# Retention followed by a GELU MLP on one core: output matmuls one MLP step later, v scaled a stage sooner, and a reordered start

## The chip, the cores and the metric

The kernel runs on one core of a Trainium2 chip. The metric is the time of one execution on the device in microseconds; the profile's span is about 1.7 us shorter than the time of the same execution.

## The reference

```python
# q, k, v: (8, 8, 576, 64); w_in: (512, 2048); w_out: (2048, 512)
def attention(q, k, v):
    scores = np.matmul(q, k.transpose(0, 1, 3, 2)) / np.sqrt(64)
    gamma = 1.0 - 2.0 ** (-5.0 - np.arange(8))
    rel = pos[:, None] - pos[None, :]
    Dmat = np.where(rel >= 0, gamma[:, None, None] ** rel, 0.0)
    return np.matmul(scores * Dmat, v)

x = attention(q, k, v).transpose(0, 2, 1, 3).reshape(4608, 512)
h = x @ w_in
g = 0.5 * h * (1.0 + erf(h / sqrt(2)))
out = g @ w_out
```

## The kernel before

The attention is done in 40 chunks of up to 128 positions (5 per batch, the last of each has 64). The decay is folded into v (`dv`) and into the result (`dq`), and what earlier chunks contribute is carried in a state `u`. TensorE does the chunks in pieces between the steps of the MLP. An MLP step is 4 matmuls of 512 columns, 0.863 us.

The names of the pieces: T turns q and k (on TensorE for chunks 0 to 8, by a DMA transpose for the others), R is the chunk's scores (tile `sc`), S its output matmuls (into `o_ps`) and its state update (`u_ps`), U the cross part (q times the state, into the same `o_ps`), X the transpose of the result for chunks 0 to 8 (`x_ps`).

```python
ps_sc  = ... bufs=2   # scores
ps_out = ... bufs=1   # o_ps: ONE buffer
ps_u   = ... bufs=1
ps_mlp = ... bufs=3

def turn(i):                      # T, chunks 0 to 8
    ...
    nc.scalar.copy(qkT[:, 1, :, :cs], ps[:, 1, :, :cs])          # k on ACT
    nc.vector.tensor_copy(qkT[:, 0, :, :cs], ps[:, 0, :, :cs])   # q on DVE

def masked(i, sc):                # DVE, after the scores
    for e in range(2):
        ...                       # ret[e] = sc[e] * mask
    vh = ...                      # vh = v * dv
    nc.vector.tensor_tensor(vh[:cs], loaded[i][1][:cs], dv[...], op=ALU.mult)

def evacuate(i):                  # DVE: x = o_ps * dq, frees o_ps
    ...
```

The order of all this is fixed when the program is built: a planner keeps an estimate `now` of TensorE's time, issues whichever piece of attention is due, and fills in MLP steps otherwise.

```python
elif kind == "R":
    sc = scores(i)
    ...
    if open_ is not None:
        cross(open_)              # the cross part of the chunk before
    masked(i, sc)                 # DVE: ret, ret, vh
    at["S", i] = now + 1.5        # S is due two MLP steps later
    if open_ is not None:
        close(open_)              # DVE: x of the chunk before, after ret, ret, vh
elif kind == "S":
    inner(i)                      # needs ret, vh, and o_ps, that is x of the chunk before
    ...
```

## Time and profile before

| | before |
|---|---|
| time, median of 3 | 338.66 us (338.36 to 339.65) |
| span of the profiled run | 337.3 us |
| TensorE (PE) busy | 309.6 us, 92% |
| idle before `o_ps` for DVE's x, PE's waits | 9.8 us, 17 times |

These lines are of the page of the kernel before: busy time by engine, then the busy share in 40 slices of the span (9 is 90% or more), the granted TensorE clock and the DMA engines' share.

```profile
span 337.3 us, 6099 instructions
PE 309.6 (92%) x2494; PEld 163.2 (48%) x2494; DVE 101.1 (30%) x183; ACT 144.8 (43%) x284; POOL 112.0 (33%) x144
PE   6879998877999999999999999999999999999995
PEclk9799999999999999999999999999999999999999
DMA  9999999999999999999979799836421120111011
```

TensorE is the bottleneck, with weaker stretches in the first quarter. The DMA engines are 90% busy or more until about 168 us. The waits of PE in the kernel before follow, an excerpt of the view (engine, line, what released it: us in total, times, the longest).

```profile
PE o_ps L236 <- DVE x L264: 9.8, 17, 0.6
PE x_ps L278 <- DVE x L264: 4.9, 5, 1.5
PE sc_1451 L208 <- DMA qkT<-qk_ld: 1.1, 1, 1.1
PE sc_1318 L208 <- DMA qkT<-qk_ld: 0.8, 1, 0.8
PE sc_1233 L208 <- DMA qkT<-qk_ld: 0.5, 1, 0.5
```

Next, one chunk of the steady state in the kernel before, from PE's timeline (start, duration, operation, and in brackets the idle time before it) ...

```profile
189.49 0.28 PE L256 MATMUL o_ps<-u_sb,qkT 64*128 64x64 bf16 x8
189.70 0.39 PE L303 MATMUL oT<-w_out_177,g_2606 128*128 128x512 bf16 x1
...
191.01 0.38 PE L303 MATMUL oT<-w_out_183,g_2674 128*128 128x512 bf16 x1
191.22 0.38 PE L303 MATMUL oT<-w_out_183,g_2681 128*128 128x512 bf16 x1
192.23 0.19 PE L236 MATMUL o_ps<-vh,ret_2795 128*128 128x64 bf16 x1 [0.63 <-DVE x L264]
```

... and what DVE does in the same stretch.

```profile
189.69 0.69 DVE L217 TENSOR_TENSOR ret_2795<-sc_2777,msk 128x512 bf16<-128x512 f32 x1 [6.23 <-PE sc_2778 L208]
190.29 0.68 DVE L217 TENSOR_TENSOR ret_2797<-sc_2778,msk 128x512 bf16<-128x512 f32 x1
190.89 0.68 DVE L221 TENSOR_TENSOR vh<-v_ld,dv 128x512 bf16<-128x512 bf16 x1
191.49 0.68 DVE L264 TENSOR_TENSOR x<-o_ps,dq 128x512 bf16<-128x512 f32 x1
```

The four DVE operations start 0.60 us apart; the output matmuls at 192.23 wait for the last one, x, which frees the one `o_ps`. Between the scores and that moment PE has only two MLP steps, eight matmuls.

The idle column says 0.63 us. But eight matmuls that start 0.216 us apart would be done issuing at 189.70 + 8 × 0.2158 = 191.43, and the next group starts at 192.23: that is 0.80 us of lost starts. The idle column counts from the modelled end of the last matmul (191.22 + 0.38 = 191.60), and a matmul's duration of 0.38 us is longer than the 0.216 us after which the next may start. The views also print no idle time under 0.15 us, so that a wait counted from start to start has to pass about 0.3 us before it shows at all.

### The profile page before, as it was taken

Reading aid. Unit: us, or ns where it says so; the run is one execution under the profiler, and the core shown is the slowest. Engines: PE = TensorE matmul, PEld = TensorE weight load, DVE = VectorE, ACT = ScalarE, POOL = GpSimd, SP = SyncE. Lnnn points to the kernel's source line nnn. Section 1 sums busy time; section 2 is a strip of 40 time slices with the busy share of each in tenths; the row PEclk is TensorE's granted clock in tenths of the full one; section 3 lists DMA queues with packets and bytes.
Section 4 is the critical chain, followed back from the end, with each engine's and each line's share of the span. In section 5 each row is a group of like instructions: output and inputs, shape, how many; then the busy total and the mean of one; then the engine's idle time right before and its main releaser. Section 6 shows DMA issues by size and latency. Waiting matters only on the chain.

```text
span 337.3 us, 6099 instructions
## 1 busy us (share of the span) xinstructions
PE 309.6 (92%) x2494; PEld 163.2 (48%) x2494; DVE 101.1 (30%) x183; ACT 144.8 (43%) x284; POOL 112.0 (33%) x144
## 2 busy tenths in 40 slices
PE   6879998877999999999999999999999999999995
PEld 2568645765544444444444444444444444444442
DVE  1751236456242223322252222322253222000000
ACT  5368425755324641464136423642354236424711
POOL 9957878544462373243334322200000000000000
PEclk9799999999999999999999999999999999999999
DMA  9999999999999999999979799836421120111011
GB/s 139 154 191 186 185 144 191 143 138 142 156 137 173 191 147 154 174 181 109 134 137 136 54 154 159 96 57 111 109 33 23 64 79 18 23 62 64 0 61 64
DMA packets 168492, 39.40 MB, mean 117 GB/s; under 512 B 157584, under 2 KB 163984, under 8 KB 168464
## 3 DMA queue, kind: packets, MB, share of 16 engines
q0 software_dynamic: 115792, 17.97, 79.6%
q1 hardware_dynamic: 52528, 20.92, 34.1%
q8 instruction: 19, 0.31, 0.4%
q10 hardware_dynamic: 144, 0.13, 0.1%
q14 instruction: 9, 0.07, 0.1%
HBM read 36.70 MB, written 9.44 MB: 137 GB/s over the span
## 4 chain that ended last, share of the span: by engine, by line
PE 70%; DVE 16%; DMA 7%; issue 5%; ACT 2%; DVEq 0%; SPq 0%; ACTq 0%
PE oT L303 30%; PE hT L290 28%; DMA qkT<-qk_ld 6%; DVE vh L221 5%; PE o_ps L236 4%; DVE x L264 4%; PE u_ps L242 2%; DMA k_101<-in_k_dram 1%; ACT qkT L197 1%; PE x_ps L278 1%; PE qk_ps L196 1%; PE o_ps L256 1%; DVE qkT L198 1%; PE warm L403 0%; ACT L172 0%
## 5 line engine op out<-in xcount | busy, mean ns | idle before, releaser
L316 ACT COPY o_sb<-oT 128x512 f32<-128x512 f32 x35 | 20.3, 586 | 77.4 <-PE oT L303 77.4
L131 POOL DMA_DIRECT2D v_ld<-in_v_dram x39 | 33.0, 845 | 55.2 <-DVE vh L221 27.5
L131 POOL DMA_DIRECT2D qk_ld<-in_q_dram x39 | 33.3, 855 | 31.7 <-DMA qkT<-qk_ld 19.3
L131 POOL DMA_DIRECT2D qk_ld<-in_k_dram x39 | 33.1, 848 | 15.1 <-DMA v_ld<-in_v_dram 13.2
L246 ACT CAST u_sb<-u_ps 128x512 bf16<-128x512 f32 x32 | 18.7, 585 | 41.4 <-PE u_ps L242 41.4
L264 DVE TENSOR_TENSOR x<-o_ps,dq 128x512 bf16<-128x512 f32 (+1 forms) x40 | 27.3, 683 | 7.7 <-PE o_ps L256 4.3
L221 DVE TENSOR_TENSOR vh<-v_ld,dv 128x512 bf16<-128x512 bf16 x31 | 21.1, 682 | 0.0
L208 PEld LDWEIGHTS <-qkT 64*128 64x128 bf16 (+1 forms) x320 | 9.2, 97 | 19.3 <-issue 12.5
L290 PE MATMUL hT<-xT,w_in_164 128*128 128x512 bf16 (+3 forms) x96 | 17.8, 326 | 0.5 <-ACT g_1133 L294 0.5
L290 PE MATMUL hT<-xT,w_in_156 128*128 128x512 bf16 (+3 forms) x96 | 18.2, 326 | 0.0
L290 PE MATMUL hT<-xT,w_in_160 128*128 128x512 bf16 (+3 forms) x96 | 18.1, 326 | 0.1
L290 PE MATMUL hT<-xT,w_in_158 128*128 128x512 bf16 (+3 forms) x96 | 17.9, 326 | 0.2 <-ACT g_1211 L294 0.2
L290 PE MATMUL hT<-xT,w_in_166 128*128 128x512 bf16 (+3 forms) x96 | 17.9, 326 | 0.0
L290 PE MATMUL hT<-xT,w_in_170 128*128 128x512 bf16 (+3 forms) x96 | 17.7, 326 | 0.1
L290 PE MATMUL hT<-xT,w_in_162 128*128 128x512 bf16 (+3 forms) x96 | 17.7, 326 | 0.0
L290 PE MATMUL hT<-xT,w_in_168 128*128 128x512 bf16 (+3 forms) x96 | 17.6, 326 | 0.1
L312 DVE COPY o_sb<-oT 128x256 f32<-128x256 f32 x1 | 0.4, 424 | 46.5 <-ACT o_sb L311 46.5
L242 PE MATMUL u_ps<-vh,qk_ld 128*128 128x128 bf16 x128 | 12.6, 222 | 0.0
L290 PEld LDWEIGHTS <-w_in_168 128*128 128x128 bf16 x96 | 8.7, 98 | 6.7 <-issue 0.2
L290 PEld LDWEIGHTS <-w_in_164 128*128 128x128 bf16 x96 | 8.6, 98 | 6.8 <-issue 0.6
L290 PEld LDWEIGHTS <-w_in_170 128*128 128x128 bf16 x96 | 8.6, 98 | 6.6 <-issue 0.2
L290 PEld LDWEIGHTS <-w_in_160 128*128 128x128 bf16 x96 | 8.5, 98 | 6.6 <-issue 0.2
(782 smaller groups left out, 626.3 us busy)
## 6 DMA issues: line engine op xcount, KB each, us to landing
out_dram<-o_sb SPq DMA_DIRECT2D x35, 256.0 KB, 2.3
qk_ld<-in_q_dram POOLq DMA_DIRECT2D x31, 128.0 KB, 8.1
qk_ld<-in_k_dram POOLq DMA_DIRECT2D x31, 128.0 KB, 7.8
v_ld<-in_v_dram POOLq DMA_DIRECT2D x31, 128.0 KB, 8.4
qk_ld<-in_q_dram POOLq DMA_DIRECT2D x8, 64.0 KB, 8.4
qk_ld<-in_k_dram POOLq DMA_DIRECT2D x8, 64.0 KB, 8.2
v_ld<-in_v_dram POOLq DMA_DIRECT2D x8, 64.0 KB, 7.5
qkT<-qk_ld SPq DMA_TRANSPOSE x31, 7.6
```

What stands on the lines that cost most here:

```text
L131: nc.gpsimd.dma_start(dst[:cs], src[b, :, c0:c0 + cs, :].rearrange("h s d -> s h d"))
L196: nc.tensor.transpose(ps[:, j, hp, :cs], qk[:cs, j, 2 * hp:2 * hp + 2, :], ident[:cs, :cs])
L197: nc.scalar.copy(qkT[:, 1, :, :cs], ps[:, 1, :, :cs])
L208: nc.tensor.matmul(sc[e][:cs, hp, :cs], lhsT=qkT[sl, 1, hp, :cs], rhs=qkT[sl, 0, hp, :cs], start=True, stop=True)
L221: nc.vector.tensor_tensor(vh[:cs], loaded[i][1][:cs], dv[:cs, :, ci:ci + 1].to_broadcast([cs, H, D]), op=ALU.mult)
L236: nc.tensor.matmul(ov[:, e, hp, :], lhsT=s["ret"][e][:, hp, :], rhs=s["vh"][:, 2 * hp + e, :], start=(hp == 0), stop=(ci == 0 and hp == HP ...
L242: nc.tensor.matmul(u_ps[0][:, hp, :], lhsT=loaded[i][0][:cs, 1, 2 * hp:2 * hp + 2, :], rhs=s["vh"][:cs, 2 * hp:2 * hp + 2, :], start=(ci = ...
L246: nc.scalar.copy(u, u_ps[0])
L264: nc.vector.tensor_tensor(x.rearrange("p hp e d -> p e hp d")[:cs], by_parity(s["o_ps"])[:cs], dq.rearrange("p (hp e) c -> p e hp c", e=2) ...
L290: nc.tensor.matmul(hT[:, :hi - lo], lhsT=w[:, cc, o:o + 128], rhs=xT[:, cc, tok0 + lo:tok0 + hi], start=(cc == 0), stop=(cc == N_DM - 1))
L303: nc.tensor.matmul(oT, lhsT=g_tiles[t, m][:, ts * 128:(ts + 1) * 128], rhs=w_out_sb[m // 2][:, m % 2, :], start=(m == 0), stop=(m == N_DF ...
L316: nc.scalar.copy(o_sb, oT)
```

## The change

Its intent is to remove the waits of the steady state (a third MLP step ahead of the output matmuls, and vh out of the DVE chain), and to shorten the dependent chain of the first chunks, before MLP work is there to fill in.

```diff
+    warm_act = const_pool.tile([128, 1], FP32, name="warm_act")   # moved up, ahead of the loads
+    nc.scalar.activation(warm_act, ln_scale, AF.Gelu)
...
-    dma_clock = [2.4]
+    dma_clock = [2.0]
...                                    # the planner's estimates of load times
-        dma_clock[0] = max(dma_clock[0], now) + 2.75 * cs / C
+        dma_clock[0] = max(dma_clock[0], now) + 3.0 * cs / C
...                                    # and 1.3 -> 1.38 for a weight tile, twice
             nc.scalar.copy(qkT[:, 1, :, :cs], ps[:, 1, :, :cs])
-            nc.vector.tensor_copy(qkT[:, 0, :, :cs], ps[:, 0, :, :cs])
+            if i in (1, 2):
+                nc.scalar.copy(qkT[:, 0, :, :cs], ps[:, 0, :, :cs])
+            else:
+                nc.vector.tensor_copy(qkT[:, 0, :, :cs], ps[:, 0, :, :cs])
+            scaled_v(i)
...
+    def scaled_v(i):                  # was the end of masked()
         vh = ...
...
-        if open_ is not None and (nxt["R"] == N_CH or (open_ < N_PE_TR and r_at > now + 1.2)):
+        if open_ is not None and (nxt["R"] == N_CH or open_ < 4 or (open_ < N_PE_TR and r_at > now + 1.2)):
...
                 inner(i)
                 nxt["S"] += 1
+                if N_PE_TR <= i + 1 < N_CH:
+                    scaled_v(i + 1)
...
-                at["S", i] = now + 1.5
+                at["S", i] = now + (1.5 if i < 4 else 2.5)
```

More of the change, by code (lines that the diff above doesn't have):

```diff
@@ L145, in load_w_in @@
         w_in_sb.append(t)
-        dma_clock[0] += 1.3
+        dma_clock[0] += 1.38
         land_in.append(dma_clock[0] + 0.8)
@@ L155, in load_w_out @@
         w_out_sb.append(t)
-        dma_clock[0] += 1.3
+        dma_clock[0] += 1.38
         land_out.append(dma_clock[0] + 0.8)
@@ L169 @@
         load_chunk(i)
-    warm_act = const_pool.tile([128, 1], FP32, name="warm_act")
-    nc.scalar.activation(warm_act, ln_scale, AF.Gelu)
     st = {i: {} for i in range(N_CH)}
@@ L219, in masked @@
             st[i]["ret"].append(r)
+    def scaled_v(i):
+        b, ci, c0, cs = chunks[i]
         vh = vh_short if cs < C else v_pool.tile([128, H, D], BF16, tag="vh", name="vh")
```

## The prediction

> **What bounds the kernel.** TensorE work: the page's busy table gives PE 309.6 of 337.3 us (92%). In the pure MLP stretches that end the chain of waits, 64 matmuls of 512 columns take 13.81 us, 215.8 ns each; the Trainium skill, "TensorE: Matmul & The Clock Gate", section "Wait — 56ns, not 53.3ns?", has 215.7 ns for a warm array. The MLP cannot be packed tighter; only PE gaps can go. In PE's timeline the gaps over 0.1 us sum to about 22.5 us:
> - 0 to 22 us: 6.9 (waits on DVE or ACT, the largest 1.48 and 1.05 for x, 1.39 for qkT);
> - 22 to 62 us: 2.75 (x_ps behind x 1.05 and 1.16; qkT 0.27 twice);
> - 62 to 90 us: 4.1 (qkT transposes by DMA 2.4; x 1.08; ACT's 64-column gelus 0.67);
> - 90 to 290 us: fifteen waits of o_ps for DVE x, 0.49 or 0.63 each, 8.75 in sum.
>
> **Steady state.** After a chunk's scores DVE runs ret, ret, vh, x (0.60 us each, start to start). PE fills this with two MLP steps (8 matmuls, 1.73 us), then waits for x, because o_ps has one buffer. The change takes vh out of that chain (-0.60) and puts a third MLP step (0.86 us) ahead of the output matmuls. Slack becomes about +0.8 us, so all fifteen waits vanish: -8.7 us. vh runs in DVE's idle time (DVE 30% busy).
>
> **First chunks.** Gelu's table load (1.28 us) moves ahead of the k cast into idle ACT time: ACT's k copy starts near 6.65 instead of 7.32. With vh off the ret chain, q copies of chunks 1 and 2 on ACT (0.58 instead of 0.42, but not behind DVE's queue), and cross closing each chunk before the next scores, I follow the durations through: chunk 1's output matmuls at about 13.5 (before 14.69), chunk 2's 16.5 (18.46), first MLP matmul 17.8 (19.46), chunk 3's output matmuls 19.8 (22.22) with equal MLP work done: -2.4 us. Landings in the trace (v of chunk 3 at 15.6; w_in from 16.9 to 26.5) just allow it.
>
> **Middle.** x_ps waits shrink from 2.2 to about 0.9, the two x waits (1.08) go: -2.4 us. But until about 150 us the DMA engines are 90% busy or more, and a qkT transpose lands 8 to 11.5 us after issue. The new order puts chunks 9 to 13 later in PE's work, about as much as PE gains, so qkT waits stay at 2 to 3 us. The 64-column gelus now run sixteen in a row: +0.4.
>
> **Sum (an estimate from these durations):** 338.7 - 8.7 - 2.4 - 2.4 + 0.5 = 325.7 us.
>
> Predicted 325.8 us, range 323.0 to 329.5 (8 in 10). Chances: faster by over 2% 0.95, within 2% 0.05, slower by over 2% 0.0.
>
> **What would show it.** PE busy stays near 309 us, its share rises to about 95%. In the waits, o_ps behind x falls from 9.8 us to under 0.5. In the timeline the first hT matmul starts near 17.8, chunk 3's output matmuls near 19.8. The tail of three pure MLP stages keeps its length. vh leaves the chain of waits (5.0% before).
>
> **What would make it wrong.** (1) DMA: if qkT doesn't land earlier, the middle keeps its absolute time and up to 4 us of early gains turn into qkT waits (330). (2) DVE runs in order: vh moved sooner can block it until v lands. (3) The half-clock stretch (8.56 to 11.97) may vanish or lengthen: about 0.6 us. (4) A later x could delay xT; I read ample lead.

## The result, and the profile after

The changed kernel takes 317.39 us (median of 4 runs, 317.04 to 318.05) against 338.62 us before (median of 4, one more than in the first table). The ratio is 0.937, with a 95% interval of 0.9345 to 0.9395. All ratios here are the mean time of one kernel's runs over that of the other's of the same rounds, so not quite the ratio of the medians. The gain is 21.2 us where 12.9 were predicted, and the time lies outside the predicted range.

The same lines of the page, for the kernel after:

```profile
span 316.3 us, 6068 instructions
PE 302.2 (96%) x2460; PEld 164.1 (52%) x2495; DVE 100.0 (32%) x181; ACT 145.0 (46%) x286; POOL 112.2 (35%) x144
PE   7889998999999999999999999999999999999995
PEclk9999999999999999999999999999999999999999
DMA  9999999999999999999999999804340221110011
```

35 matmul records are missing from this trace (2460 matmuls for 2495 weight loads), so its PE busy time is not to be compared with the other. PE's waits in the kernel after, again an excerpt:

```profile
PE x_ps L284 <- DVE x L270: 0.7, 2, 0.4
PE hT L296 <- DMA w_in_160<-in_moe_w_in_dram: 0.7, 1, 0.7
PE sc_1578 L211 <- DMA qkT<-qk_ld: 0.6, 1, 0.6
PE sc_1699 L211 <- DMA qkT<-qk_ld: 0.5, 1, 0.5
```

The wait of `o_ps` for x is gone from the list. The same chunk in PE's timeline of the kernel after (one of the twelve matmuls has no record) ...

```profile
175.59 0.28 PE L262 MATMUL o_ps<-u_sb,qkT 64*128 64x64 bf16 x8
175.81 0.39 PE L309 MATMUL oT<-w_out_179,g_2608 128*128 128x512 bf16 x1
...
178.19 0.38 PE L309 MATMUL oT<-w_out_194,g_2751 128*128 128x512 bf16 x1
178.41 0.19 PE L242 MATMUL o_ps<-vh,ret_2799 128*128 128x64 bf16 x1
```

... and DVE's part of it, where vh comes last and nobody waits for it:

```profile
175.79 0.69 DVE L220 TENSOR_TENSOR ret_2799<-sc_2781,msk 128x512 bf16<-128x512 f32 x1 [5.91 <-PE sc_2782 L211]
176.40 0.68 DVE L220 TENSOR_TENSOR ret_2801<-sc_2782,msk 128x512 bf16<-128x512 f32 x1
177.00 0.68 DVE L270 TENSOR_TENSOR x<-o_ps,dq 128x512 bf16<-128x512 f32 x1
177.59 0.68 DVE L227 TENSOR_TENSOR vh<-v_ld,dv 128x512 bf16<-128x512 bf16 x1
```

From 175.81 to 178.41 are 2.60 us for twelve matmuls, and 12 × 0.2158 is 2.59: no start is lost.

Where did 21 us come from? I lined up the two traces with the programs' order of matmuls and, for each stretch, took the distance between the starts of its groups less what the matmuls need at their undisturbed spacing (0.2158 us at 512 columns, 0.109 at 256, and so on). This counts every lost start, whatever the modelled ends say.

| term | predicted, us | measured start to start, us |
|---|---|---|
| output matmuls' waits after 87 us (26 in the kernel before) | -8.7 | -13.6 (13.9 to 0.3) |
| start, to the end of the first MLP stage | -2.4 | -2.6 (37.60 to 34.95) |
| output matmuls' waits in the middle | -1.1 | -2.0 (2.0 to 0.0) |
| `x_ps` waits in the middle | -1.3 | -1.5 (2.5 to 1.0) |
| waits for landings of qkT and of q | 0 | -1.2 (2.9 to 1.7) |
| 64-column stage, bound by ACT | +0.4 | -0.7 (2.1 to 1.4) |
| sum | -13.1 | -21.6 (spans: -21.0) |

The terms overshoot the spans by 0.6 us: small ones that are not listed go the other way, such as 0.35 us between the first two score matmuls of one chunk at 64.50 us in the kernel after. The 0.3 that is left of the first term is 0.01 us at each group, as in e2 below, and no wait.

The largest error is the first line. The profile booked the 26 late waits of the kernel before as fifteen: ten of 0.63 us and five of 0.49. Start to start they are ten of 0.80, five of 0.67, five of 0.32 and six of 0.15 us, 13.9 us in all. The five of 0.32 leave 0.15 us of idle time, just under what the views print, and the six of 0.15 leave none.

### The profile page after: what moved, and what is told of

It is laid out like the page before. It is cut to its first block, busy times and chain, and to the rows that moved or that the text cites. A ratio compares the mean times of both kernels' runs of the same rounds, so it can differ in the third digit from the quotient of the medians.

```text
span 316.3 us, 6068 instructions
## 1 busy us (share of the span) xinstructions
PE 302.2 (96%) x2460; PEld 164.1 (52%) x2495; DVE 100.0 (32%) x181; ACT 145.0 (46%) x286; POOL 112.2 (35%) x144
## 4 chain that ended last, share of the span: by engine, by line
PE 86%; DMA 6%; POOL 3%; ACT 2%; issue 1%; DVE 1%; ACTq 0%
PE hT L296 39%; PE oT L309 36%; DMA qkT<-qk_ld 3%; PE o_ps L242 3%; DMA w_in_160<-in_moe_w_in_dram 2%; PE u_ps L248 2%; POOL qk_ld L134 2%; PE o_ps L262 2%; POOL v_ld L134 1%; ACT o_sb L322 0%; PE x_ps L284 0%; PE qk_ps L195 0%; DVE x L270 0%; ACT qkT L196 0%; DVE qkT L200 0%
## 5 line engine op out<-in xcount | busy, mean ns | idle before, releaser
L134 POOL DMA_DIRECT2D qk_ld<-in_q_dram x39 | 33.4, 856 | 50.7 <-DMA qkT<-qk_ld 18.3
L211 PEld LDWEIGHTS <-qkT 64*128 64x128 bf16 (+1 forms) x320 | 9.4, 97 | 16.3 <-issue 12.7
```

What stands on the lines that cost most here:

```text
L134: nc.gpsimd.dma_start(dst[:cs], src[b, :, c0:c0 + cs, :].rearrange("h s d -> s h d"))
L211: nc.tensor.matmul(sc[e][:cs, hp, :cs], lhsT=qkT[sl, 1, hp, :cs], rhs=qkT[sl, 0, hp, :cs], start=True, stop=True)
```

## The experiments

Three theories are set against each other. Theory S: waits must be read start to start, and each is the DVE chain less the MLP work that covers it. Rival I: the idle column is what can be gained, and the extra gain has another source. Rival D: that source is the planner's new DMA constants, which move chunks 9 to 13 relative to the MLP. For the start the question is, part by part, whether it is on the critical path at all. Twelve kernels ran, all correct. For comparisons between kernels of different rounds I give the ratio; the changed kernel's is 0.937.

| run | what | median, us | ratio to before (95%) |
|---|---|---|---|
| e1_vh_only | before, with vh sooner | 325.49 | 0.9602 (0.9548 to 0.9655) |
| e2_step_only | before, with the third step | 320.36 | 0.9446 (0.9403 to 0.9489) |
| e3_first_only | before, with all the rest | 337.49 | 0.9949 (0.9900 to 0.9998) |
| e4_vh_step | before, with vh and step | 319.38 | 0.9415 (0.9372 to 0.9459) |
| e5_no_cross | after, cross late again | 319.15 | 0.9419 (0.9403 to 0.9434) |
| e6_no_split | after, q copies on DVE | 318.49 | 0.9401 (0.9387 to 0.9416) |
| e7_no_table | after, table load late | 317.28 | 0.9369 (0.9354 to 0.9383) |
| e8_no_clock | after, old DMA constants | 317.88 | 0.9375 (0.9355 to 0.9396) |
| e9_no_vh | after, vh late again | 319.65 | 0.9445 (0.9417 to 0.9474) |
| e10_one_step | before, one step only | 366.29 | 1.0827 (1.0794 to 1.0859) |
| e11_four_steps | after, a fourth step | 320.38 | 0.9454 (0.9420 to 0.9489) |
| e12_thirds | after, no 64-column stage | 317.01 | 0.9362 (0.9340 to 0.9383) |

### e1: vh alone

```diff
-    (end of masked)  vh = v * dv
+    scaled_v(i): in turn(i) for chunks 0 to 8, after inner(i - 1) for the others
```

> The kernel before with one part alone: v is scaled a stage sooner. Theory S (waits must be read start to start: before, 26 output-matmul groups after 87 us each start late, ten by 0.80, five by 0.67, five by 0.32, six by 0.15 us, 13.9 us in all): taking vh's 0.60 us out of the chain cuts each by at most 0.60, so about 11.5 us there, plus some 3.5 us from the x waits and output waits of the first 87 us: 323 to 324 us, and in the late part ten waits of 0.20 and five of 0.07 remain. Rival I (the idle column is the loss: fifteen waits, 8.75 us): at most 8.5 us there and about 2.5 earlier: 327 to 328 us.

325.49 us: slower than theory S said and faster than rival I. The late part settles it. PE's waits view lists nothing at all for the stretch from 85 to 279 us, yet the timeline of this kernel reads:

```profile
181.98 1.90 PE L307 MATMUL oT<-w_out,g 128*128 128x512 bf16 x8
183.91 0.39 PE L240 MATMUL o_ps<-vh,ret 128*128 128x64 bf16 x8
```

From 181.98 to 183.91 is 1.93 us for eight matmuls that need 1.73: a wait of 0.20, as predicted (0.80 less 0.60). The last matmul's duration hides all but 0.03 us of it, and the view doesn't list so little. The ten long waits are 0.20 each and the five next 0.07, and the late part lost 11.5 us, exactly theory S's number. What is missing is in the middle, where waits for DMA grew:

```profile
PE sc L209 <- DMA qkT<-qk_ld: 4.6, 4, 1.5
```

Before, they were 2.4 us by the same column (2.9 start to start; here 5.2). TensorE came earlier to scores whose transposes had not landed. So over 2 us of vh's gain were given back to the DMA queues.

### e2: the third MLP step alone

```diff
-                at["S", i] = now + 1.5
+                at["S", i] = now + (1.5 if i < 4 else 2.5)
```

> The kernel before with one part alone: output matmuls one MLP step later for chunks 4 and up. An MLP step is 0.863 us, more than the longest late wait. Theory S: all 26 late waits vanish, 13.9 us, and about 2.5 us of output waits between 37 and 87 us; waits of x_ps stay. 321 to 323 us. Rival I: 8.75 us late and 1.1 in the middle: 328 to 329 us.

320.36 us, a little better than theory S said and 8 us better than rival I. The late waits are 0.01 us each. Two lines of this kernel's page and waits show more. First the busy line:

```profile
PE 304.5 (95%) x2494; PEld 164.1 (51%) x2494; DVE 101.0 (32%) x183; ACT 144.1 (45%) x284; POOL 112.0 (35%) x144
```

This kernel has the same matmuls as the one before and as many records (2494), but PE busy fell from 309.6 to 304.5 us. Busy time had contained about 5 us of waiting: the drain of the last matmul before each wait. Second, the waits for qkT:

```profile
PE sc L208 <- DMA qkT<-qk_ld: 0.6, 1, 0.6
```

They fell from 2.4 to 0.6 us, where vh alone raised them to 4.6. A later S puts the following chunk's R later in TensorE's work too, so the transposes have more time to land. The traces show it: the MLP work done before the scores of chunks 10 to 13, counted in matmuls of 512 columns, is 154, 164, 172 and 180 in the kernel before and in e1, but 158, 170, 182 and 196 in e2. The prediction had expected these waits to stay.

### e3: all the rest, alone; e4: vh and step together

```diff
 e3: at["S", i] = now + 1.5, vh in masked(); the other parts of the change
 e4: the two steady-state parts; nothing of the start, old DMA constants
```

> The kernel before with everything but the two steady-state parts: cross at once for chunks 0 to 3, the q copies of chunks 1 and 2 on ACT, Gelu's table sooner, the planner's new DMA constants; vh stays late and no step is added. Theory S (the extra gain of the middle, 6 us from 35 to 77 us, comes from output waits that the two other parts take away): 336 to 337 us, a gain of 1.5 to 2.5 us at the start and next to none in the middle. Rival D (the new DMA constants, which put chunks 9 to 13 later in TensorE's work, give the extra gain of the middle): 332 to 334 us.

> The kernel before with both steady-state parts and none of the others. Theory S: 13.9 us late, about 2.5 us from x_ps waits, 2.5 us from output waits in the middle, little at the start: 319 to 321 us. Rival D: the middle keeps its qkT waits (3 us) and some more: 322 to 324 us. Neither theory lets it reach the changed kernel's 317.4.

e3 took 337.49 us and e4 319.38 us, 1.1 and 19.2 us less than before. e4 lies where theory S put it; e3 is 0.5 us above its range. The middle of e4 improves without the new constants, so rival D finds nothing here. The late gains of e1 and e2 overlap: both take away the same waits. That is why 13.1 (vh) and 18.3 (step) add up to only 19.2.

### e5, e6, e7, e8: the parts of the start and the constants, each undone in the changed kernel

```diff
 e5: -  open_ < 4 or ...
 e6: -  if i in (1, 2): nc.scalar.copy(...)        all q copies on DVE
 e7: -  warm_act ahead of the loads                 back behind the k cast
 e8: -  dma_clock 2.0, 3.0, 1.38                    back to 2.4, 2.75, 1.3
```

> The changed kernel with its cross-at-once part undone: chunks 1 and 2 are closed after the next chunk's scores again. Theory S: x of chunks 1 and 2 leaves DVE behind both ret again, up to 0.6 us each, part of it hidden under the wait for the second w_in tile (0.68 us in the changed kernel): 317.9 to 318.6 us. Rival: nothing of the start is on the critical path, since the weights' landing holds the first MLP steps anyway: 317.4.

> The changed kernel with all q copies on DVE again. A copy takes 0.42 us on DVE and 0.59 on ACT, but on DVE it queues with ret and vh. Theory S: chunk 2's scores wait for DVE, 0.2 to 0.5 us in all: 317.6 to 317.9 us. Rival (the copies on ACT only cost time, 0.17 each): 317.1 us.

> The changed kernel with Gelu's table load back behind the k cast. Theory S: the first k copy starts some 0.65 us later and the chain of the first chunks with it; the weight wait of 0.68 us absorbs part: 317.6 to 318.1 us. Rival: all is absorbed, 317.4.

> The changed kernel with the planner's old DMA constants (2.4, 2.75, 1.3), which put chunks 5 to 13 earlier in TensorE's work. Theory S (output waits were the bulk of the middle's gain; scores meet a qkT that has not landed only somewhat more): 318 to 319.5 us, the excess in scores' waits for qkT by DMA. Rival D (the constants gave most of what the middle gained beyond the forecast, 4 us): 320.5 to 322 us.

Without cross at once the ratio is 0.9419, worth about 1.7 us; without the split of the copies 0.9401, about 1.1 us. Both are more than I had expected. The first stands clear of the noise. The second is at its edge: the intervals overlap (0.9387 to 0.9416 against 0.9345 to 0.9395), though all four runs of e6 (318.14 us and up) are slower than all four of the changed kernel (318.05 us and below). The rival that gave cross at once nothing falls, and so does the one that had the copies on ACT only cost time. The table load gives nothing measurable (0.9369): the 0.65 us are absorbed, as its rival said; in the changed kernel the first MLP steps wait 0.7 us for a weight tile anyway, and in e7 that wait is gone from PE's list. The DMA constants give nothing measurable either (0.9375). Rival D falls, and so does my own smaller expectation of 0.6 to 2.1 us.

### e9: vh late again, with the third step kept

```diff
-  scaled_v(i), scaled_v(i + 1)
+  vh at the end of masked(), as before
```

> The changed kernel with vh back behind the two ret. The third MLP step (0.863 us) alone covers the longest late wait (0.80), by a margin of 0.06. Theory S: late waits stay under 1 us in sum; the first chunks and x_ps lose up to 0.6 us at four or five places: 318.5 to 320 us. Rival (both parts are needed in the steady state, each giving its own 0.6 or 0.86 us): 323 us or more.

319.65 us. The 28 late waits sum to 0.3 us, so in the steady state vh's move is redundant once the third step is there. By the ratio it is still worth about 2.5 us. The traces place 1.2 us of that at `x_ps`; the rest lies in the first chunks as far as can be told, where the two traces differ in the clock as well. These are PE's waits in this kernel after 53 us; the first line was 0.7 in the changed kernel:

```profile
PE x_ps L281 <- DVE x L267: 1.9, 2, 1.0
PE sc L211 <- DMA qkT<-qk_ld: 0.9, 3, 0.4
```

### e10: one MLP step fewer than before

```diff
-                at["S", i] = now + 1.5
+                at["S", i] = now + (1.5 if i < 4 else 0.6)
```

> The kernel before with one MLP step fewer between a chunk's scores and its output matmuls (chunks 4 and up): the same work, the same chain on DVE, 0.863 us less cover. Theory S (each late wait is the DVE chain less the cover, counted start to start): every one of the 26 late waits grows by 0.86 us, 22 us late, and some 3 to 4 us more for the chunks in the middle: 361 to 366 us, late waits of 1.66, 1.53, 1.18 and 1.02 us. Rival (waits are made of something else, DMA or clock, and cover does not matter): under 350 us.

366.29 us, 0.3 us above the range. The late waits are ten of 1.66, five of 1.53, five of 1.18 and six of 1.02 us: each of the 26 grew by 0.86, one step's worth, 22.4 us in all. In the timeline of this kernel:

```profile
206.00 1.04 PE L303 MATMUL oT<-w_out,g 128*128 128x512 bf16 x4
208.53 0.39 PE L236 MATMUL o_ps<-vh,ret 128*128 128x64 bf16 x8 [1.49 <-DVE x L264]
```

Start to start it is 2.53 less 0.86, 1.67 us by these rounded starts; the idle column again has 0.17 to 0.18 less. With e1, e2 and this run the wait is measured in four cases (the chain shortened by 0.60, its cover of MLP work longer by 0.86, the cover shorter by 0.86, and both as they were), and one sum fits all of them to 0.02 us. No run gave `o_ps` a second buffer, the obvious other cure for the waits that end at x.

### e11: a fourth step

```diff
-                at["S", i] = now + (1.5 if i < 4 else 2.5)
+                at["S", i] = now + (1.5 if i < 4 else 3.4)
```

> The changed kernel with a fourth MLP step before the output matmuls. Theory S: there is no late wait left to cover, so the late part stays as it is to 0.5 us; only the order in the middle can move: 316.5 to 318.5 us. Rival (later output matmuls gain by themselves, by easing the DMA queues or otherwise): 315.5 us or less.

320.38 us, about 3 us slower than the changed kernel: a miss. No late output wait was left to cover, but the results of each chunk come later, and one MLP stage now comes up before its input has landed and has to wait:

```profile
96.47 2.12 PE L297 MATMUL hT<-xT,w_in 128*128 128x512 bf16 x6 [2.87 <-issue]
```

The view names no releaser. The trace has the DMA transpose of x of the last chunk that this stage needs landing at 96.38. In the changed kernel that transpose lands at 93.97 and the stage starts at 96.03, so the lead is only 2.1 us. The idle stretch then costs a second time, in the clock (PEclk of the windows before and after; columns as in the first line):

```profile
core 0: us, PE busy (x) PEld busy (x) DVE busy (x) ACT busy (x) POOL busy (x), PEclk, DMA share, GB/s
92.50:97.00 4.50, 1.63 (x29) 1.03 (x28) 2.48 (x4) 0.58 (x1) 3.29 (x4) 1.00 1.56 189
97.20:100.50 3.30, 3.30 (x9) 1.11 (x8) 0.00 (x0) 1.19 (x2) 0.89 (x2) 0.50 1.58 200
```

Half clock from 97.1 for 3.4 us loses another 1.7 us of starts. This part is not in every run: the one run with a mean granted clock of 0.999 took 318.59 us, the three at 0.994 or 0.995 took 320.30 to 321.05.

### e12: an attempt at a better version

```diff
-        cuts = {0: (0, 256, 512), 1: (0, 192, 448, 512)}.get(t, (0, 512))
+        cuts = {0: (0, 256, 512), 1: (0, 192, 384, 512)}.get(t, (0, 512))
```

> The changed kernel with block 1's first MLP half cut at 192, 384, 512 tokens instead of 192, 448, 512: no 64-column stage, whose gelus take ACT about 0.22 us each against 0.12 us of matmuls and cost some 1.5 us of waits in the changed kernel. If that reading is right, 0.8 to 1.5 us faster than the changed kernel: 316.0 to 316.6 us. If the qkT landings hold the same stretch, the gain turns into waits for them: 317.4.

317.01 us, ratio 0.9362; the interval overlaps that of the changed kernel, so no gain is shown. PE's wait for ACT's gelus is gone from its list, but the waits for qkT are larger (1.1 in the changed kernel):

```profile
PE sc L212 <- DMA qkT<-qk_ld: 1.5, 2, 1.3
```

Of the two outcomes written down this is the second, that what is gained there turns into waits for landings; but this view shows only 0.4 us more of them, so the rest is not accounted for.

## Why the prediction was wrong

- **What bounds the kernel, and which waits go:** right. TensorE is the bottleneck; the fifteen waits of `o_ps` for x vanished, and the tail of three pure MLP stages kept its 45.3 us.
- **The size of the late term:** wrong, and this is the step that failed. The prediction said "fifteen waits of o_ps for DVE x, 0.49 or 0.63 each, 8.75 in sum", and "-8.7 us". The runs show 26 waits and 13.9 us, of which 13.6 went. The idle column starts at the modelled end of the last matmul, 0.165 us after the next could have started, and the views print nothing under 0.15 us of idle time: eleven waits of 0.15 to 0.32 us were not seen at all. e1, e2 and e10 confirm the start-to-start sizes to 0.02 us. Of the 8.3 us that the prediction missed (21.2 less 12.9), this term is 4.9. The same reading took 0.9 us off the output waits in the middle.
- The information was at hand. The Trainium skill, "TensorE: Matmul & The Clock Gate", section "Single matmul latency", gives a warm matmul (398 + N)/2.4 ns, 379 ns at N = 512, where the section that the prediction names has a spacing of 215.7 ns; this trace has 0.38 us and 215.8 ns. The skill's "Trainium Kernel Development and Optimization", section "Performance Expectations", warns that matmul busy time is a bad metric because matmuls are pipelined. The prediction cited the spacing and still subtracted idle time that was measured from the latency's end. e2's busy line puts the error at 5 us of "busy" waiting.
- **qkT waits:** wrong. "The new order puts chunks 9 to 13 later in PE's work, about as much as PE gains, so qkT waits stay at 2 to 3 us." With the landing of one q they fell from 2.9 to 1.7 us. The third step spaces the scores (e2: 0.6 us by the waits view), vh alone would have made them worse (e1: 4.6 us), and the new constants were not the reason (e8).
- **The 64-column stage:** the sign was wrong, by 1.1 us (+0.4 predicted, -0.7 measured). The matmuls of this stage wait for ACT's gelus in both kernels, 1.8 us before and 1.4 after. The other 0.3 is an output wait for x that fell into this stage before.
- **The start:** right in size (-2.4 against -2.6), with output matmuls of chunk 3 at 19.9 us (19.8 predicted), but not in its parts, so that the agreement is in part luck. The first MLP matmul came at 16.9 instead of 17.8 us and then waited for a weight tile; the table load gave nothing (e7); cross at once and the split gave about 1.7 and 1.1 us (e5, e6).
- **vh in the steady state:** the prediction let both parts add up to a slack of 0.8 us. That is true and harmless, but vh's part of it buys nothing once the step is there (e9).
- **"A later x could delay xT; I read ample lead":** the change itself was not hurt, but the lead was 2.1 us at the tightest stage, and e11 shows it gone with one more step.

What stays open is how much of the start's gain is the clock, and how large that part is from run to run. The kernel before had half clock from 8.6 to 12.0 us, and so had e1, e2 and e4, which start like it. But e10 starts like it too and had none, and its first MLP stage began 0.95 us sooner (18.5 against 19.5 us). The kernel after had half clock until 7.0 us by the spacing of its matmuls, e9 and e11 only until 4.5 and 5.0, and e3 until 10.4 us, which weighs on its small gain. The clocks size the part that they show: of the 23 executions of the kernel before that the experiments list, the 11 with a mean granted clock of 0.998 or more have a median of 338.49 us, the 12 below it 339.19. That is a difference of 0.7 us, against a gain of 21.2. The half clock before the first recorded change does not show in these clocks, and no run separates its effect from that of the change.

## What to carry to other kernels

Size a wait of TensorE from start to start: the distance between the first starts of two groups, less the number of matmuls times their undisturbed spacing. The idle column is short by the drain of one matmul at each wait (0.165 us here), and waits of up to 0.32 us were missing from the view, so many small bubbles can be worth half again what it shows. When a wait is a chain on another engine less the work that covers it, one more covering step can be better than a shorter chain, since it also gives later loads time to land; but check the lead of whatever the covered work feeds, because the next step too many is paid there.

## What the Trainium skill lacked or had wrong

- "TensorE: Matmul & The Clock Gate", section "Back-to-back issue gap", gives about 131 ns per matmul as the sustained rate at N = 512 in a stream of weight loads and matmuls, and calls 216 ns the isolated gap. Here 64 such pairs take 13.81 us, 215.8 ns each; the measurement decides.
- "Perfetto Trace Analysis", section "Optimization Strategy", tells to find the gaps between slices on the bottleneck engine. It doesn't say that on TensorE a gap is short by the drain (0.165 us here) and that a wait of about that size leaves next to none: in e1 ten waits of 0.20 us left 0.03 us each.
- The same section says that consistent bubbles can mean too little SBUF or PSUM for the next tile. The trace fits that for the fifteen long waits, which end at x, the reader of the one buffer of `o_ps`; no run here tried a second buffer. It doesn't name the other cure, more covering work (e2, 18 us).
- "TensorE: Matmul & The Clock Gate", section "What's actually happening", says that the clock gate's window of 3413 ns runs free, so the warm-up varies. The traces agree: half-clock stretches of 3.41 us came at 8.6 us (before), at 89.3 us (e10) and at 97.1 us after a wait of 2.9 us (e11), and starts alike ran with and without one. In a start like this one it came to 0.95 us, between the profiled runs of e10 and of the kernel before.
- The profile's clock is not reliable before its first recorded change: in e3 PEclk reads 1.00 from 8.6 to 10.3 us, while three matmuls of 512 columns took 1.42 us there (0.82 in the kernel after); the first recorded change of e3 is at 10.4 us. The same page warns of such records in general.
- I found no page with the time that a DMA transpose takes to land beside other loads: the 31 of qkT in the kernel after took 8.5 us in the median, up to 12.7 us.
